# The turned v of a fused attention and feed-forward kernel: from TensorE to transposing DMAs, and the pace of the second half's units

## Chip, cores and metric

The kernel runs on one core of one Trainium2 chip. The metric is the device time of one execution in microseconds (us), lower being better. The kernel before was timed five times; its median is 241.97 us, and the five times lie between 241.94 and 242.24 us.

## What is computed

The reference first turns `sort_net` into one 8x8 block-mixing matrix P for each of the 32 heads (4 batches of 8 heads). It then mixes the eight 96-row blocks of k and v with P, runs softmax attention block by block, and feeds the result to a bilinear feed-forward layer:

```
P: five times exp, then rows and columns divided by their sums
k_sorted = einsum('bhij,bhjcd->bhicd', P, k_blocks)     # 8 blocks of 96 rows, 64 wide
v_sorted = einsum('bhij,bhjcd->bhicd', P, v_blocks)
attn     = softmax(scale * q_block @ k_sorted_block.T)  # 96 x 96 for each block
o        = attn @ v_sorted_block
x        = o with heads side by side                    # 3072 tokens x 512
out      = ((x @ w_a) * (x @ w_b)) @ w_out              # 512 -> 1536 -> 512
```

## The kernel before

**Tiling.** Heads are worked on in pairs: a pair's two 64-wide heads fill 128 partitions. There are 16 pairs, numbered g = 0 to 15, four to a batch. A pair passes through stage c (mix k and v), stage s (scores and exp) and stage o (attention times v, division by the row sums). Four finished pairs make up xT, the transposed input of one batch's feed-forward layer. A step `ffn_ab` of that layer is eight 384-column matmuls on TensorE (four with w_a, four with w_b), a copy of the first product by ScalarE and a multiply by VectorE; `ffn_out` multiplies with w_out and stores.

**What v needs.** The mix gives v with the head dimension on the partitions (vT). The o matmul wants the 96 tokens of a block on the partitions (vs), so every block of vT is transposed. The kernel before does it in two ways. For batch 0 and for pair 4, the first pair of batch 1, TensorE does it: `half_v` (line 205) transposes four blocks of a pair into PSUM and VectorE copies them to vs (line 211); `turn_v` (line 269) does the same for all eight blocks of pair 4. For pairs 5 to 15 `return_v` (line 316) issues one transposing DMA, SBUF to SBUF, on the queue of SyncE (SP).

**Order of work.** The order on TensorE, GpSimd (POOL) and SP is the order in which the program is written. Batch 0 is treated in two halves of its blocks, h = 0 and h = 1, so that the feed-forward layer can begin early. Half 0 is written out by hand (lines 499 to 529). The twelve units of half 1 come from `units_half` (line 547) and are laid between the twelve `ffn_ab` steps of half 0 by `interleave` (line 628). For each pair hp they are: `half_scores` with `half_v` right behind it, in one unit; `half_o`; and `half_x`, which transposes the result on TensorE and copies it into xT. `half_x` of a pair is placed behind a later step than its `half_o`. With one step kept free at the end and two at the beginning, `interleave` has placed ceil((s-1) x 12 / 9) units once the step of index s is done. After that come steps that share TensorE with the pairs of batch 1 (`paced`, line 637, in the order of line 604: c4, s4, c5, s5, c6, o4, s6 ...). The last two unit kinds wait for other engines: `half_o` for ScalarE's exp (line 202), `half_x` for VectorE's reciprocal and multiply (lines 237 and 239).

**Buffers.** There are four vT tiles, one for each pair of a batch, and three vs tiles used in turn (g modulo 3). In the PSUM pool psF, four banks serve the feed-forward products, the transposes of v and x, and the first mixes.

**DMA.** POOL issues all loads with a cast to bf16 (`load_ab` line 105: w_a and w_b in six column chunks of 256, two steps of the layer each; `load_pair` line 88; `load_out` line 111: w_out in three parts). SP issues the stores and the transposing DMAs: `stage_q` (line 252) for the q of later pairs, `return_v`, and `to_xT` (line 341). SP takes them strictly in turn, and each waits there for its inputs.

Of the kernel before, what the change touches and what calls it, by code (L numbers as in the profile page):

```python
# [10 lines left out]
BF16 = mybir.dt.bfloat16  # L11
# [11 lines left out]
def kernel(  # L23
# [11 lines left out]
    nc = tc.nc  # L35
    P = 128
    B, H, S, D = q.shape
    NB = sort_net.shape[-1]
    BLK = S // NB
# [7 lines left out]
    HP = H // 2  # L47
    KA = DMODEL // P
    KO = DFF // P
    NBH = NB // 2  # L50
# [4 lines left out]
    V0 = 16  # L55
# [12 lines left out]
    psF = ctx.enter_context(tc.tile_pool(name="psF", bufs=4, space=PSUM))  # L68
# [5 lines left out]
    ident = const.tile([P, P], BF16, name="ident")  # L74
# [50 lines left out]
    NBUF = 3  # L125
    kTs = [const.tile([P, S + PAD], BF16, name=f"kT{n}") for n in range(HP)]
    vTs = [const.tile([P, NB, P], BF16, name=f"vT{n}") for n in range(HP)]
    eTs = [const.tile([BLK, 2, 2, HB + PAD], BF16, name=f"eT{n}") for n in range(NBUF)]
    vss = [const.tile([P, NB, VW], BF16, name=f"vs{n}") for n in range(NBUF)]
# [29 lines left out]
    def copy(eng, out, in_):  # L159
        if eng == "act":  # L160
            nc.scalar.copy(out=out, in_=in_)  # L161
        else:
            nc.vector.tensor_copy(out=out, in_=in_)  # L163

    def keep_busy(ps, n, cols=512):
        for _ in range(n):
            nc.tensor.matmul(ps[:, 0:cols], lhsT=warm[:, 0:P], rhs=warm[:, 0:cols],  # L167
                             start=True, stop=True)


    def mix_mms(g, what, where):
        src2 = loaded[g][0 if what == "k" else 1]
        for c in range(NCH):
            for e in range(2):
                nc.tensor.matmul(where(c)[e * D:(e + 1) * D], lhsT=src2[:, e, c * D:(c + 1) * D],  # L175
                                 rhs=s_all[:, 2 * g + e], start=True, stop=True)

    def mix_first(g, what, engines, fill=0, cols=512):
        mix = [psF.tile([P, 512], FP32, tag="F", name="mixf") for _ in range(2)]
        keep_busy(mix[0], fill, cols)  # L180
        mix_mms(g, what, lambda c: mix[c // 3][:, c % 3 * P:(c % 3 + 1) * P])
        for u, eng in enumerate(engines):
            copy(eng, turned(g, what, u),
                 _ap(mix[u], 0, [[512, P], [P, 3], [CG, NB], [1, CG]]))

    def turned(g, what, u):
        if what == "k":
            return _ap(kTs[g % HP], u * 3 * CG, [[S + PAD, P], [CG, 3], [BLK, NB], [1, CG]])
        return _ap(vTs[g % HP], u * 3 * CG, [[NB * P, P], [CG, 3], [P, NB], [1, CG]])

    def half_scores(h, hp):
        g = h * HP + hp
        kT, qT, eT = kTs[hp], st[hp, "qT"], eTs[g % NBUF]
        sc = psA.tile([P, 2, 512], FP32, tag="A", name="sc")
        for i in range(NBH):
            for e in range(2):
                nc.tensor.matmul(  # L197
                    sc[:, e, i * BLK:(i + 1) * BLK],
                    lhsT=kT[e * D:(e + 1) * D, (h * NBH + i) * BLK:(h * NBH + i) * BLK + P],
                    rhs=qT[e * D:(e + 1) * D, :, (h * NBH + i) * CG:(h * NBH + i + 1) * CG],  # L200
                    start=True, stop=True)
        nc.scalar.activation(out=eT[:, 0, :, 0:HB], in_=sc[0:BLK, :, 0:HB],  # L202
                             func=AF.Exp, scale=float(scale))

    def half_v(h, hp):
        g = h * HP + hp
        vT, vs = vTs[hp], vss[g % NBUF]
        vs_ps = psF.tile([P, NBH, 2, D], BF16, tag="F", name="vs_ps")
        for i in range(NBH):
            nc.tensor.matmul(vs_ps[:, i], lhsT=vT[:, h * NBH + i], rhs=ident, is_transpose=True)  # L210
        nc.vector.tensor_copy(out=vs[0:BLK, 0:NBH, V0:V0 + P],
                              in_=vs_ps[0:BLK].rearrange("p i e d -> p i (e d)"))

    def half_o(h, hp):
        g = h * HP + hp
        xp = att.tile([BLK, NBH, 2, D], BF16, tag="xph", name="xph")
        one_o(eTs[g % NBUF], 0, vss[g % NBUF], 0, xp, NBH)
        st["x", h, hp] = xp

    def half_x(h, hp, eng):  # L220
        xT, xp = xT_of(0), st["x", h, hp]
        xt_ps = psF.tile([P, NBH, BLK], BF16, tag="F", name="xt_ps")
        for i in range(NBH):
            nc.tensor.matmul(xt_ps[:, i, :], lhsT=xp[:, i],  # L224
                             rhs=ident[0:BLK, 0:BLK], is_transpose=True)
        copy(eng, xT[:, hp, h * HW:(h + 1) * HW].rearrange("p (i t) -> p i t", i=NBH), xt_ps)
# [30 lines left out]
    def turn_q(g, eng="dve"):  # L257
# [7 lines left out]
        qT = qtp.tile([P, NCH, P], BF16, tag="qT", name="qT")  # L265
        copy(eng, qT, q_ps)
        st[g, "qT"] = qT

    def turn_v(g):
        vT, vs = vTs[g % HP], vss[g % NBUF]  # L270
        vs_ps = psF.tile([P, NB, P], BF16, tag="F", name="vs_ps")
        for i in range(NB):
            nc.tensor.matmul(vs_ps[:, i], lhsT=vT[:, i], rhs=ident, is_transpose=True)
        nc.vector.tensor_copy(out=vs[0:BLK, :, V0:V0 + P], in_=vs_ps[0:BLK])

    def stage_k(g):
        mix = psA.tile([P, 2, 512], FP32, tag="A", name="mix")
# [13 lines left out]
    def plain(g):  # L291
        return g >= 2 * HP + 2
# [23 lines left out]
    def return_v(g):  # L316
        nc.sync.dma_start_transpose(out=vss[g % NBUF][:, :, V0:V0 + P],
                                    in_=vTs[g % HP].rearrange("p i t -> p (i t)"))
# [105 lines left out]
    with tc.manual_schedule(engines={ET.PE, ET.Pool, ET.SP}):  # L424
        with tc.manual_schedule(engines={ET.Activation, ET.DVE}):
# [7 lines left out]
            for it in range(5):  # L433
# [8 lines left out]
                if it == 2:  # L442
                    with nc.allow_low_precision("sum of one one and zeros"):
                        nc.vector.reduce_sum(
                            out=mask, in_=_ap(ident, 0, [[P, P], [1, CG], [CG, NB]]),
# [14 lines left out]
                else:  # L460
                    nc.vector.tensor_mul(
                        out=p_fin.bitcast(BF16).rearrange("h (i j u) -> h i j u", i=NB, j=NB),
# [30 lines left out]
            def partial(n, *kcs):  # L493
                if n not in begun:
                    begun[n] = (psF.tile([P, 512], FP32, tag="F", name="pf") if n < 3 else
                                psA.tile([P, 2, 512], FP32, tag="A", name="two")[:, 0])
                ab_mms(begun[n], (w_a_sb, w_b_sb)[n % 2], 0, n // 2, 0, kcs)
# [3 lines left out]
            mix_first(1, "v", ("act", "dve"), 1)  # L501
            mix_first(1, "k", ("act", "dve"))
            half_scores(0, 0)
            half_v(0, 0)
            mix_first(2, "v", ("act", "dve"))
            mix_first(2, "k", ("act", "act"))
            half_o(0, 0)
            half_scores(0, 1)
            half_v(0, 1)
            half_v(0, 2)  # L510
            mix_first(3, "k", ("dve", "act"))
            half_scores(0, 2)
            half_o(0, 1)
            mix_first(3, "v", ("act", "act"))
            half_x(0, 0, "dve")
            half_o(0, 2)
            half_x(0, 1, "act")
            half_scores(0, 3)
            partial(0, 0)
            half_v(0, 3)  # L520
            partial(0, 1)
            half_x(0, 2, "dve")
            half_o(0, 3)
            partial(4, 0, 1, 2)
            partial(2, 0, 1, 2)
            partial(0, 2)
# [18 lines left out]


        def units_half():
            def R(hp):
                half_scores(1, hp)
                half_v(1, hp)  # L550

            us = []
            for hp in range(HP):
                us.append(lambda hp=hp: R(hp))
                if hp > 0:
                    us.append(lambda hp=hp: half_x(1, hp - 1, "dve"))
                us.append(lambda hp=hp: half_o(1, hp))
            us.append(lambda: half_x(1, HP - 1, "dve"))
            return us

        def c_(g):
            if g < 2 * HP - 2:
                turn_q(g)
            if plain(g):
                stage_plain(g, "k", ("act",))
                stage_plain(g, "v", ("dve", "act"))
            else:
                stage_k(g)
                stage_v(g)
            if plain(g):  # L570
                pair_q(g)
                stage_q(g)
            else:
                if g > HP:
                    return_v(g)
                if g >= 2 * HP - 2:
                    nc.gpsimd.tensor_copy(out=gate, in_=kTs[g % HP][0:1, 0:1])  # L577
                    load_later(g)

        def s_(g):  # L580
            stage_scores(g)
            if g == HP:
                turn_v(g)
            if g in (HP, HP + 1):
                stage_q(g + 2)
            if 2 * HP <= g + 1 < B * HP and not plain(g + 1):
                pair_q(g + 1)
                stage_q(g + 1)
# [20 lines left out]
        for n, (b, u, g) in enumerate(seq):  # L609
            if u is c_ and plain(g):  # L610
                late = 3 if g % HP == 0 else 2
                after[n + 1] += [lambda g=g, what=what: in_order(g, what) for what in "kv"]
                if late == 3:
                    after[n + 3].append(lambda g=g: nc.gpsimd.tensor_copy(
                        out=gate, in_=xT_of(g // HP - 1)[0:1, HP - 1, 0:1]))
# [8 lines left out]
        units = [[] for _ in range(B)]  # L624
# [3 lines left out]
        def interleave(steps, units, spare, first):  # L628
            n, done = len(steps) - spare - first, 0
            for s, step in enumerate(steps):  # L630
                step()
                want = -(-(s + 1 - first) * len(units) // n)
                while done < min(want, len(units)):
                    units[done]()
                    done += 1
# [53 lines left out]
```

The softmax here doesn't subtract the row's maximum and nothing guards it: scores larger than these inputs give would overflow.

## Time and profile before

| | |
|---|---|
| median of five runs | 241.97 us |
| the profiled execution's own time | 242.03 us |
| its span, first to last instruction | 240.2 us |
| TensorE (PE) busy | 233.7 us, 97% of the span |
| VectorE (DVE), ScalarE (ACT) busy | 111.2 us and 101.3 us |
| transposing DMAs on SP's queue | 45: 11 vs, 10 q, 12 k and v of later pairs, 12 xT |
| `half_v`: PE transposes, DVE copies | 32 of 219 ns each, 8 of 416 ns each |
| `turn_v`: PE transposes, DVE copy | 8 of 220 ns each, 1 of 687 ns |

About 1.8 us of the execution lie outside the span. PE is matmul, PEld the loading of weights into TensorE ahead of a matmul. Matmuls overlap in TensorE, so 219 ns is how long one took from start to end; how long it holds up the next is read from the distance of starts. "Waits" tell which engine or DMA ended an engine's idle time, and "issue" is time for which the profile shows no cause. "To landing" is the time from a DMA's issue to its completion. All times are counted from the start of the span.

### The profile page before, as it was taken

To read this page: it belongs to the slowest core of one execution; us is meant where nothing else is said; L and a number is where in the kernel's file an instruction comes from. 1 tells how busy PE (TensorE), PEld (TensorE's weight loads), DVE (VectorE), ACT (ScalarE), POOL (GpSimd) and SP (SyncE) were. 2 spreads that over 40 slices of the span, in tenths; PEclk is the share of its full clock that TensorE was granted. 3 is DMA by queue.
4 is the path that set the end of the run, shared out by engine and by line. 5 is a ranking of instruction groups with operands and counts; after the bars stand their busy time and mean duration, and the time that the engine had idled before them with its cause. 6 is when DMAs were issued, how large, how long until landed. Compare 5 with 4: busy or idle time off the path is not lost.

```text
span 240.2 us, 5193 instructions
## 1 busy us (share of the span) xinstructions
PE 233.7 (97%) x2091; PEld 138.8 (58%) x2091; DVE 111.2 (46%) x262; ACT 101.3 (42%) x187; POOL 70.4 (29%) x97
## 2 busy tenths in 40 slices
PE   7899899999999999999999999999999999999994
PEld 7776566666554466666645455666544466665443
DVE  6797667546345144365406244644544134444110
ACT  3774634664630165743640356455500133333001
POOL 8776569623320055071620515411000000000000
PEclk9999999999999999999999999999999999999999
DMA  5999999995998589769995899975325200000132
GB/s 77 202 199 196 196 200 201 202 166 98 151 151 205 125 120 160 120 104 197 155 202 109 160 252 100 151 142 35 76 61 140 101 30 3 0 0 3 44 130 88
DMA packets 63527, 30.35 MB, mean 126 GB/s; under 512 B 40336, under 2 KB 60560, under 8 KB 63504
## 3 DMA queue, kind: packets, MB, share of 16 engines
q0 software_dynamic: 20944, 14.16, 42.2%
q1 hardware_dynamic: 42416, 15.81, 34.2%
q8 instruction: 16, 0.26, 0.4%
q10 hardware_dynamic: 144, 0.07, 0.1%
q14 instruction: 7, 0.06, 0.1%
HBM read 28.32 MB, written 6.29 MB: 144 GB/s over the span
## 4 chain that ended last, share of the span: by engine, by line
PE 92%; DVE 4%; ACT 1%; DMA 1%; issue 1%; DVEq 0%; ACTq 0%
PE pf L357 52%; PE po L402 24%; PE o_ps L233 3%; PE sc L327 2%; PE mix L175 2%; PE mix L298 2%; PE mixf L175 1%; PE po L387 1%; PE sc L197 1%; PE vs_ps L210 1%; DMA p_nat<-in_sort_net_dram 1%; PE xt_ps L224 1%; DVE csum L455 1%; PE two L357 1%; DVE xp L239 1%
## 5 line engine op out<-in xcount | busy, mean ns | idle before, releaser
L378 DVE TENSOR_TENSOR hT<-a_sb,pf 128x384 bf16<-128x384 bf16 x95 | 52.6, 553 | 71.6 <-PE pf L357 45.2
L357 PE MATMUL pf<-xT,w_a_sb 128*128 128x384 bf16 x380 | 78.0, 326 | 0.0
L357 PE MATMUL pf<-xT,w_b_sb 128*128 128x384 bf16 x380 | 77.4, 326 | 0.0
L377 ACT CAST a_sb<-pf 128x384 bf16<-128x384 f32 x95 | 45.4, 479 | 63.2 <-PE pf L357 39.9
L402 PE MATMUL po<-w_out_sb,hT 128*128 128x512 bf16 x276 | 61.9, 379 | 0.0
L357 PEld LDWEIGHTS <-w_b_sb 128*128 128x128 bf16 x384 | 37.5, 98 | 24.7
L357 PEld LDWEIGHTS <-w_a_sb 128*128 128x128 bf16 x384 | 35.3, 98 | 22.4
L402 PEld LDWEIGHTS <-hT 128*128 128x128 bf16 x276 | 26.2, 97 | 30.2
L161 ACT COPY o_sb<-po 128x512 f32<-128x512 f32 (+1 forms) x13 | 7.5, 578 | 48.9 <-PE po L402 47.5
L163 DVE COPY o_sb<-po 128x512 f32<-128x512 f32 (+1 forms) x12 | 7.9, 658 | 38.7 <-PE po L402 34.1
L332 ACT ACTIVATE eT<-sc 96x768 bf16<-96x768 f32 x24 | 18.1, 802 | 5.2 <-PE sc L327 5.2
L239 DVE TENSOR_TENSOR xp<-o_ps,rec 96x512 bf16<-96x512 f32 x24 | 15.9, 684 | 0.3
L314 POOL COPY kT<-turned 128x768 bf16<-128x768 bf16 x6 | 5.0, 827 | 33.5 <-DMA turned<-nat 28.0
L233 PEld LDWEIGHTS <-eT 96*128 96x128 bf16 x256 | 10.2, 97 | 4.4 <-ACT eT L202 1.1
L96 POOL DMA_DIRECT2D k<-in_k_dram x16 | 11.6, 724 | 3.5 <-PE pf L357 1.3
L96 POOL DMA_DIRECT2D v<-in_v_dram x16 | 11.6, 722 | 2.8 <-DMA w_b_sb<-in_moe_w_b_dram 1.3
L233 PE MATMUL o_ps<-vs,eT 96*128 96x65 bf16 x256 | 11.4, 193 | 1.0 <-ACT eT L202 0.6
L577 POOL COPY gate<-kT 1x1 bf16<-1x1 bf16 x4 | 0.7, 178 | 32.2 <-ACT kT L280 27.7
L161 ACT CAST nat<-mix 128x768 bf16<-128x768 f32 (+1 forms) x12 | 7.7, 639 | 4.2 <-PE mix L298 2.5
L248 POOL COPY qc<-q 128x768 bf16<-128x768 bf16 x10 | 8.5, 846 | 2.6 <-DMA q<-in_q_dram 2.6
L96 POOL DMA_DIRECT2D q<-in_q_dram x12 | 8.7, 724 | 1.5 <-DMA w_a_sb<-in_moe_w_a_dram 0.6
L167 PE MATMUL heat<-warm 128*128 128x128 bf16 x84 | 7.4, 259 | 1.3 <-DVE warm L77 1.3
(86 smaller groups left out, 163.8 us busy)
## 6 DMA issues: line engine op xcount, KB each, us to landing
out_dram<-o_sb SPq DMA_DIRECT2D x17, 256.0 KB, 2.0
k<-in_k_dram POOLq DMA_DIRECT2D x16, 192.0 KB, 5.5
v<-in_v_dram POOLq DMA_DIRECT2D x16, 192.0 KB, 6.1
q<-in_q_dram POOLq DMA_DIRECT2D x12, 192.0 KB, 6.5
w_a_sb<-in_moe_w_a_dram POOLq DMA_DIRECT2D x6, 256.0 KB, 9.0
w_b_sb<-in_moe_w_b_dram POOLq DMA_DIRECT2D x6, 256.0 KB, 9.5
w_out_sb<-in_moe_w_out_dram POOLq DMA_DIRECT2D x3, 512.0 KB, 12.1
out_dram<-o_sb SPq DMA_DIRECT2D x12, 128.0 KB, 2.4
```

The lines of the kernel that those rows point to most:

```text
L96: nc.gpsimd.dma_start(out=to, in_=_ap(t, base, [[W, P], [S * D, 2], [1, W]]))
L161: nc.scalar.copy(out=out, in_=in_)
L163: nc.vector.tensor_copy(out=out, in_=in_)
L167: nc.tensor.matmul(ps[:, 0:cols], lhsT=warm[:, 0:P], rhs=warm[:, 0:cols], start=True, stop=True)
L233: nc.tensor.matmul(o_ps[:, e, i * (D + 1):(i + 1) * (D + 1)], lhsT=eT[:, hf, e, i * BLK:i * BLK + P], rhs=vs[0:BLK, i0 + i, V0 - 1 + e * ( ...
L239: nc.vector.tensor_tensor(out=_ap(xp, i0 * 2 * D, [[nxp * 2 * D, BLK], [D, 2], [2 * D, NBH], [1, D]]), in0=_ap(o_ps, 1, [[1024, BLK], [511 ...
L248: nc.gpsimd.tensor_copy(out=qc.rearrange("p c e d -> p e c d"), in_=loaded[g][2].rearrange("p e (c d) -> p e c d", c=NCH))
L332: nc.scalar.activation(out=eT[:, hf, :, 0:HB], in_=sc[0:BLK, :, 0:HB], func=AF.Exp, scale=float(scale))
L357: nc.tensor.matmul(pf[:, 0:HW], lhsT=w_sb[:, kc, m * P:(m + 1) * P], rhs=x_cols(b, kc, t), start=(kc == 0), stop=(kc == KA - 1))
L377: nc.scalar.copy(out=a_sb, in_=pf[:, 0:HW])
L378: nc.vector.tensor_mul(out=hT[:, m, t * HW:(t + 1) * HW], in0=a_sb, in1=ab[1][:, 0:HW])
L402: nc.tensor.matmul(held["po"], lhsT=hTs[b][:, m, c * P:(c + 1) * P], rhs=w_out_sb[:, m, :], start=(m == 0), stop=(m == KO - 1))
```

## The change

Half 1 of batch 0: the new `second_v(hp)` issues one transposing DMA on SP's queue, which turns blocks 4 to 7 of the pair's vT into the vs tile that half 1 of the pair will read. It is issued as soon as the previous reader of that vs tile has been written down: `second_v(0)`, `(1)` and `(2)` behind `half_o(0, 1)`, `(0, 2)` and `(0, 3)` in the hand-written part, `second_v(3)` behind `half_o(1, 0)`. The four `half_v(1, hp)` are gone. Pair 4: `turn_v` is gone, and `return_v(4)` is issued in stage c like those of the later pairs. The units of half 1 are in a new order, in which scores run one pair ahead, and `interleave` rounds the number of units down where it rounded up.

```diff
+    def second_v(hp):
+        nc.sync.dma_start_transpose(out=vss[(HP + hp) % NBUF][:, 0:NBH, V0:V0 + P],
+                                    in_=vTs[hp][:, NBH:].rearrange("p i t -> p (i t)"))
+
-    def half_v(h, hp):
-        g = h * HP + hp
-        vT, vs = vTs[hp], vss[g % NBUF]
+    def half_v(hp):
+        vT, vs = vTs[hp], vss[hp % NBUF]
...
-            nc.tensor.matmul(vs_ps[:, i], lhsT=vT[:, h * NBH + i], rhs=ident, is_transpose=True)
+            nc.tensor.matmul(vs_ps[:, i], lhsT=vT[:, i], rhs=ident, is_transpose=True)
...
-    def turn_v(g):
...
             half_o(0, 1)
+            second_v(0)
             mix_first(3, "v", ("act", "act"))
             half_x(0, 0, "dve")
             half_o(0, 2)
+            second_v(1)
             half_x(0, 1, "act")
             half_scores(0, 3)
             partial(0, 0)
-            half_v(0, 3)
+            half_v(3)
             partial(0, 1)
             half_x(0, 2, "dve")
             half_o(0, 3)
+            second_v(2)
             partial(4, 0, 1, 2)
...
         def units_half():
-            def R(hp):
-                half_scores(1, hp)
-                half_v(1, hp)
-
-            us = []
+            def O(hp):
+                half_o(1, hp)
+                if hp == 0:
+                    second_v(HP - 1)
+
+            us = [lambda: half_scores(1, 0)]
             for hp in range(HP):
-                us.append(lambda hp=hp: R(hp))
+                if hp + 1 < HP:
+                    us.append(lambda hp=hp: half_scores(1, hp + 1))
                 if hp > 0:
                     us.append(lambda hp=hp: half_x(1, hp - 1, "dve"))
-                us.append(lambda hp=hp: half_o(1, hp))
+                us.append(lambda hp=hp: O(hp))
             us.append(lambda: half_x(1, HP - 1, "dve"))
             return us
...
-                if g > HP:
-                    return_v(g)
+                return_v(g)
...
             stage_scores(g)
-            if g == HP:
-                turn_v(g)
...
-                want = -(-(s + 1 - first) * len(units) // n)
+                want = (s + 1 - first) * len(units) // n
```

The units of half 1 behind each `ffn_ab` step, with S for `half_scores`, V for `half_v`, O for `half_o` and X for `half_x` (steps 0, 1 and 11 have none in either kernel):

| step | 2 | 3 | 4 | 5 | 6 | 7 | 8 | 9 | 10 |
|---|---|---|---|---|---|---|---|---|---|
| before | S0 V0 O0 | S1 V1 | X0 | O1 S2 V2 | X1 | O2 | S3 V3 X2 | O3 | X3 |
| after | S0 | S1 | O0 S2 | X0 | O1 | S3 X1 | O2 | X2 | O3 X3 |

More of the change, by code (lines that the diff above doesn't have):

```diff
@@ L267, in turn_q @@
         st[g, "qT"] = qT
-    def turn_v(g):
[L270 to L274, printed above, removed]
     def stage_k(g):
@@ L503 @@
             half_scores(0, 0)
-            half_v(0, 0)
+            half_v(0)
             mix_first(2, "v", ("act", "dve"))
@@ L508 @@
             half_scores(0, 1)
-            half_v(0, 1)
-            half_v(0, 2)
+            half_v(1)
+            half_v(2)
             mix_first(3, "k", ("dve", "act"))
```

## Prediction

> **What bounds the kernel now.** I read the page first, then the chain of waits, the timeline where the change sits, and last the DMA's landings.
>
> The page says TensorE:
>
> ```profile
> PE 233.7 (97%) x2091; PEld 138.8 (58%) x2091; DVE 111.2 (46%) x262; ACT 101.3 (42%) x187; POOL 70.4 (29%) x97
> DMA  5999999995998589769995899975325200000132
> ```
>
> PE has work in 97% of the span. The second line is the DMA's share in slices of 6 us: it is full from 6 us to about 54 us, and that is where the change puts five more transfers. So I need both: what TensorE saves, and whether the new transfers come in time on a full DMA.
>
> The chain around the first unit of half 1 (start, length, what):
>
> ```profile
> 25.36 0.36 PE sc L197 x8
> ...
> 25.80 0.81 ACT eT L202
> 26.62 0.05 issue
> 26.66 0.42 PE o_ps L233 x8
> ```
>
> S0, V0 and O0 come in one go, and O0 waits for the exp. V0 starts at 25.64 in the timeline and takes 0.23, so O0 could start at 25.87 and starts at 26.66: PE stands still for 0.79 us.
>
> The timeline of O3 and X3, with one step between them:
>
> ```profile
> 38.86 0.41 PE L233 MATMUL o_ps<-vs,eT 96*128 96x65 bf16 x8
> ...
> 39.83 0.69 DVE L239 TENSOR_TENSOR xph<-o_ps,rec 96x512 bf16<-96x512 f32 x1
> ...
> 40.57 0.20 PEld L224 LDWEIGHTS <-xph 96*128 96x128 bf16 x4 [0.39 <-DVE xph L239]
> 40.58 0.34 PE L224 MATMUL xt_ps<-ident,xph 96*128 96x96 bf16 x4
> ```
>
> From O3's start to X3's is 1.72 us: VectorE finishes a product, then the reciprocal and the multiply. O3 takes 0.25 (the step starts at 39.11) and the step 1.30, so X3 waits 0.17.
>
> The third view is the tile qTf, whose first transposing DMA met the full DMA:
>
> ```profile
> L254 SPq DMA_TRANSPOSE qTf<-qc x10: 1212/1306/2238, 42.8 to 161.1; - x10
> DMA to landing us min/median/max: 2.6/4.2/10.5
> ```
>
> The reader is to see the longest: 10.5 us from issue to landing, against a median of 4.2. It is the first of the ten, issued at 42.78 on the full DMA and landed at 53.30.
>
> [...]with nothing else under way (54.5 to 55.0 us) I count 545 packets of 256 bytes in the trace's packet records, 279 GB/s; beside the loads of w_out, 155 packets in a us, 40 GB/s. [...]from 47 to 50 us 463 of POOL's and 468 of SP's, one for one.
>
> **The change part by part.**
>
> TensorE transposes. V1 runs from 28.59 to the next step at 28.83, V2 from 32.22 to 32.45, V3 from 37.15 to 37.38, V0 took 0.23: 0.92 us of PE for four. turn_v: 46.43 to 46.89, 0.46 us. All of it is on PE, which is the bound: -1.38. The five VectorE copies that go (4 x 0.42 and 0.69 us) count 0: VectorE is busy 46% of the span and its copies lie beside PE's matmuls. If VectorE were the limit there, they would bring up to 2.4 us more.
>
> The new order. S0 and O0 are two steps apart: -0.79. S1 to S3 keep their places behind a step or an O. O0 to X0 has S2 and a step between, O1 to X1 a step and S3, 1.9 us each against the 1.4 (O0 before, VectorE free) to 1.72 that VectorE takes: 0; without S2 or S3 each would cost 0.17. O2 to X2 is now a pair like O3 and X3 before, one step apart: +0.17; the old X3 wait goes: -0.17. O3 and X3 now follow each other behind step 10, with nothing between: 1.72 less O3's own 0.25, +1.47. What is late next behind X3 is its copy into xT, which the next batch of steps reads; step 11 (1.30 us) covers it, as now.
>
> Sum for TensorE: -1.38 - 0.79 - 0.17 + 0.17 + 1.47 = -0.70. At c4 the shift is -0.24, from o4 on -0.70.
>
> SP's queue. It now holds second_v(0) to (3), then return_v(4), then stage_q(6), which stood first and went out at 42.78. An issue takes about 1.25 us of SP (the vs rows). second_v(3) waits at the head for O0; behind it there is only return_v(4), over 15 us later: 0. stage_q(6) goes behind return_v(4), at about 47.
>
> second_v in time? (0) can go when half_o(0,1) is done, 18.45; (1) 19.7; (2) 21.55; (3) about 29.2. 512 packets each. Under load the first packets came 3.4 to 3.9 us after the issue (qTf 42.78, 46.7; xT 59.67, 63.1). A transposing packet beside POOL's costs these about 1.5 ns: w_out alone goes at 200 packets a us, paired at 155 (1/155 - 1/200). The chunks of w_a and w_b go alone at 390 a us, so paired at about 243, an estimate. Then (0) lands by 25.5 and is read at O0 near 28.6; (1), (2) and (3) have 3 us and more. The change makes each O's weight load wait for these landings, and all of TensorE's later work is queued behind it, so if the slack is gone, each us late is a us lost; I take 0, with a pause of 0.85 (below) too. The copies of vT at c4 on VectorE and ScalarE now wait for the landings as well, as they overwrite what is being turned: 44 us against 25 to 35, 0.
>
> What they do to the loads. 1536 packets x 1.6 ns (1/243 - 1/390) put POOL's loads back by 2.4 us, with second_v(3) and slower pairs 3.2. The first that matters is chunk 1 of w_a: landed at 21.21, read at 21.34. A first transposing packet at 20.8 instead of 22 would cost up to 0.4; none, 0. I take 0.15. The other chunks have over 2 us, but for chunk 2 of w_b (landed 25.02, now 27.4, read about 28.1): 0, up to 0.9 with a pause. Pair 4 (36.0, read at 43.5), pair 5 and w_out have 4 us or more.
>
> return_v(4). The copies of vT (ScalarE's 45.28 + 0.48) end at 45.76, with c4's shift and w_a's wait (-0.24 + 0.15) at 45.67. Its data is read by o4, whose weights are loaded from
>
> ```profile
> 57.21 0.36 PEld L233 LDWEIGHTS <-eT 96*128 96x128 bf16 x5
> ```
>
> now at 57.21 - 0.70 + 0.15 = 56.66. Its first packets go out about 3.6 us after the issue, 49.2, when w_out is being loaded (put back by 3.2 us, to 48.0 and later). 1024 packets at 155 a us are 6.6 us, and a landing came 0.8 after the last packet: 56.6. That is just in time. But the DMA stopped in that very stretch before, and the table of stretches of 2 us shows it in its last column:
>
> ```profile
> 48.00:50.00 2.00, 2.00 (x26) 1.20 (x25) 0.79 (x2) 0.96 (x2) 1.61 (x1) 1.00 1.24 204
> 50.00:52.00 2.00, 2.00 (x36) 1.31 (x31) 1.34 (x3) 1.39 (x3) 0.00 (x0) 1.00 1.37 119
> ```
>
> 204 GB/s fall to 119: from 50.7 to 51.6 hardly a packet starts. Up to 46 us, loads alone, there was no such pause after the first 5 us; with both queues busy (46 to 54 us) there were two. I take one of 0.85 for return_v(4): +0.85, with ends 0 and 1.7.
>
> stage_q(6) follows on the same ring with 768 packets. Two us of them share with w_out's rest, the others run alone or beside pair 8's loads: it lands between 59.5 and 61.8. s6 reads it at 60.56 - 0.70 + 0.15 + 0.85 = 60.86. Cost 0 to 0.9; I take 0.40. return_v(5) and stage_q(7) then have 2 us or more.
>
> Sum: -0.70 + 0.15 + 0.85 + 0.40 = +0.70. Against the profiled execution 242.03 + 0.70 = 242.73; it lies 0.06 above the median of the runs, 241.97, so 242.67, say 242.7.
>
> **The rivals.**
>
> The crossbar keeps up. For it: 56.6 against 56.66 without a pause, and slack everywhere else. Against it: the pauses. Time: 241.97 - 0.70, with 0 to 0.15 for w_a: 241.3 to 241.4, faster. This is the one on the other side; it decides at a pause of about 0.1 us before return_v(4)'s last packet.
>
> A wait at o4 alone, part of a pause or a whole one, after which stage_q(6) is in time: for it speaks that s6 comes later by o4's wait, against it that 768 packets still stand behind return_v(4). -0.70 + 0.15 + 0.5 to 0.85, 241.9 to 242.3, no change.
>
> Late weights. Pauses come in the first stretch already, where 1536 new packets share with w_a and w_b, and chunk 2 of w_b holds up step 4: +0.9, with 0.85 at o4: 243.1 to 243.5. Against it: the small chunks have shown no pause so far, though alone.
>
> The unit order does not do what it says: "evenly" puts O3 and X3 together. That is in the sum; without it all cases were 1.47 lower.
>
> **How the numbers follow.** Forecast 0.37 (242.5 to 243.1), late weights 0.09, a wait at o4 alone 0.29, the crossbar in time 0.25. A measurement of this kernel can tell about 0.2%, 0.48 us, from no change, so the bounds are 241.49 and 242.45. Faster 0.25, same 0.29, slower 0.46. The range reaches from the fast rival's 241.3 to 243.4 and leaves out the end of the late weights and what I haven't seen. The forecast's own range is 242.45 to 243.1.
>
> **What would show it.** Right: no wait of O0 for eT; PE idle about 1.5 us before X3, released by VectorE's xph; PE waiting for the DMA vs<-vT before o4 near 57, with return_v(4) landing 11 us or more after its issue; a smaller wait before s6 for qTf<-qc. Wrong: return_v(4) landing under 10 us, or no PE wait for a DMA at all: then it is near 241.3. Also wrong if second_v's packets go out of turn with the loads, so that O0 waits for its vs, or if X3's wait is under 1 us.

## The result and the profile after

The kernel after takes 245.03 us, the median of 27 runs (242.58 to 248.88), against 242.12 for 48 runs of the kernel before (241.83 to 243.22). The ratio of the comparison is 1.0061, with a 95% interval of 1.0046 to 1.0076: slower, by more than the 0.2% that can be told from no change. That ratio leaves out the eleven runs over 246.2 us, all of them at a TensorE clock of 0.986 to 0.993 (the profile below, one of them, shows the low clock right behind the kernel's own wait); with every run the ratio of the two medians is 1.012. The forecast, 242.7 us with 241.3 to 243.4, has the right sign, and the median lies outside it.

The profiled execution took 248.75 us with a span of 246.7. It is a bad one of the 27, but the two other profiles of the same kernel (`after_again`, 245.37 us, and `after_third`, 242.65 us) show the same wait, of other lengths.

First the page of the kernel after. The last two lines are groups: busy time and mean ns, then idle time and what ended most of it.

```profile
PE 234.2 (95%) x2067; PEld 137.9 (56%) x2067; DVE 109.2 (44%) x257; ACT 100.9 (41%) x187; POOL 70.4 (29%) x97
...
PEclk9999999999799999999999999999999999999999
DMA  5999999999999949958998798953227310000132
...
L236 PE MATMUL o_ps<-vs,eT 96*128 96x65 bf16 x256 | 11.4, 193 | 4.1 <-DMA vs<-vT 3.8
...
L236 PEld LDWEIGHTS <-eT 96*128 96x128 bf16 x256 | 10.2, 97 | 7.8 <-DMA vs<-vT 4.2
```

PE falls from 97 to 95% of a longer span. The DMA is now full to about 86 us (14 slices of 6.17 us), where it was full to 54, and the o matmul waits for a DMA into vs. One slice of the clock, the 11th (62 to 68 us), isn't full.

The chain at half 1's first units, in the kernel after:

```profile
26.61 0.35 PE sc L197 x8
26.96 1.41 PE pf L353 x8
28.36 0.28 PE sc L197 x8
28.64 1.41 PE pf L353 x8
30.05 0.25 PE o_ps L236 x8
```

Where S0 was followed by 0.81 us of exp, the chain runs through TensorE alone, and O0 takes 0.25 us in place of 0.42. O0 waits neither for eT nor for the turned v.

The timeline of O3 and X3 in the kernel after:

```profile
39.89 0.41 PE L236 MATMUL o_ps<-vs,eT 96*128 96x65 bf16 x8
...
41.60 0.20 PEld L227 LDWEIGHTS <-xph 96*128 96x128 bf16 x4 [1.43 <-DVE xph L242]
41.61 0.34 PE L227 MATMUL xt_ps<-ident,xph 96*128 96x96 bf16 x4 [1.31 <-DVE xph L242]
```

From O3's start to X3's it is 1.72 us, as before, with no step between: PE is idle for 1.3 us. Of the rest of the new order only X2 holds PE up, by 0.17 us, as forecast: it starts at 38.41, 1.72 after O2.

The chain that ends at o4, in the three profiles of this kernel, first the one of the page, then `after_again`, then `after_third`:

```profile
46.82 15.03 DMA vs<-vT
61.84 0.05 issue
61.89 0.67 PE o_ps L236 x16
```

```profile
46.13 14.02 DMA vs<-vT
60.15 0.05 issue
60.19 0.67 PE o_ps L236 x16
```

```profile
45.49 11.92 DMA vs<-vT
57.41 0.05 issue
57.46 0.67 PE o_ps L236 x16
```

The middle column is return_v(4) from its issue to its landing: 15.0, 14.0 and 11.9 us. The forecast had 10.9 without a stop of the DMA and 11.8 with the one that it took, so the third profile meets it. c4 to o4 takes 13.47 us where nothing waits (44.00 to 57.47 in `rv4_only`, below). Here it takes 17.41, 16.40 and 14.30, so o4's wait costs 3.94, 2.93 and 0.83 us.

The stretches around o4 in the kernel after (busy time of PE, PEld, DVE, ACT and POOL, then the granted clock, DMA share, GB/s):

```profile
58.00:60.00 2.00, 0.12 (x1) 0.00 (x0) 0.55 (x1) 0.21 (x1) 1.97 (x3) 1.00 1.29 171
60.00:62.00 2.00, 0.11 (x4) 0.11 (x5) 0.00 (x0) 0.00 (x0) 0.00 (x0) 1.00 1.40 80
62.00:64.00 2.00, 2.00 (x22) 1.26 (x21) 1.56 (x4) 0.17 (x1) 0.00 (x0) 0.64 1.72 140
64.00:66.00 2.00, 2.00 (x8) 0.91 (x6) 0.56 (x1) 0.30 (x1) 0.00 (x0) 0.51 1.55 105
66.00:68.00 2.00, 2.00 (x26) 1.17 (x25) 0.55 (x1) 1.32 (x3) 0.00 (x0) 1.00 1.33 196
```

PE stands still for 3.8 us; then the clock is 0.50 for 3.4 us (62.5 to 66.0, in whole stretches 0.64 and 0.51), and o4 to s6 takes 4.88 us in place of 3.19. In `after_again`, where PE waits 2.8 us, the clock stays full:

```profile
58.00:60.00 2.00, 0.00 (x0) 0.00 (x0) 0.10 (x1) 0.00 (x0) 1.28 (x2) 1.00 1.43 125
60.00:62.00 2.00, 1.81 (x25) 1.29 (x25) 1.31 (x4) 0.40 (x1) 0.00 (x0) 1.00 1.33 190
```

There o4 to s6 takes 3.21 us, and 3.20 in `after_third`. So the half clock is a cost of its own, 1.69 us, which of the three profiles only the one with the longest wait shows.

The account of the page's profile against the one of before, 248.75 - 242.03 = 6.72 us: a later S0, 26.61 against 25.36, +1.25; S0 to c4 -0.22; turn_v -0.45; o4's wait +3.94; the half clock +1.69; the time from the last matmul's start to the span's end +0.2; outside the span +0.3. The sum is 6.71. The later S0 comes from the first loads: the first mixes wait for a v that lands at 16.50, before the first new transfer is even issued (19.76). In `after_third` S0 is at 25.29, and the sum there is -0.07 - 0.22 - 0.45 + 0.83 + 0.22 + 0.31 = +0.62, measured 242.65 - 242.03.

### The profile page after: what moved, and what is told of

The parts are those of the page before. It is cut to its first block, busy times and chain, and to the rows that moved or that the text cites. A ratio compares the mean times of both kernels' runs of the same rounds, so it can differ in the third digit from the quotient of the medians.

```text
span 246.7 us, 5165 instructions
## 1 busy us (share of the span) xinstructions
PE 234.2 (95%) x2067; PEld 137.9 (56%) x2067; DVE 109.2 (44%) x257; ACT 100.9 (41%) x187; POOL 70.4 (29%) x97
## 4 chain that ended last, share of the span: by engine, by line
PE 84%; DMA 10%; POOL 2%; DVE 2%; issue 0%; POOLq 0%; DVEq 0%
PE pf L353 48%; PE po L398 24%; DMA vs<-vT 6%; DMA v<-in_v_dram 4%; PE o_ps L236 3%; PE sc L323 2%; PE mix L294 2%; PE mix L175 1%; PE po L383 1%; POOL k L96 1%; PE sc L197 1%; PE xt_ps L227 1%; PE mixf L175 1%; POOL q_first L83 1%; POOL v L96 1%; PE two L353 1%
## 5 line engine op out<-in xcount | busy, mean ns | idle before, releaser
L353 PE MATMUL pf<-xT,w_a_sb 128*128 128x384 bf16 x380 | 79.1, 330 | 0.0
L240 DVE RECIPROCAL rec<-o_ps 96x8 f32<-96x8 f32 x32 | 5.6, 189 | 8.9 <-PE o_ps L236 8.7
```

What stands on the lines that cost most here:

```text
L240: nc.vector.reciprocal(out=rec, in_=_ap(o_ps, 0, [[1024, BLK], [512 + D, 2], [D + 1, NBH]]))
L353: nc.tensor.matmul(pf[:, 0:HW], lhsT=w_sb[:, kc, m * P:(m + 1) * P], rhs=x_cols(b, kc, t), start=(kc == 0), stop=(kc == KA - 1))
```

## Experiments

Three theories stood at the start. A: return_v(4) meets the load of w_out (POOL's last before the later pairs) whatever second_v does, and its landing decides o4. B: it is second_v, whose 2048 packets put the loads back, and return_v(4) comes in time without it. C: the new order of the units holds the time. After the first four runs came A2: only both together are late, since second_v puts w_out back to where it covers the whole of return_v(4)'s transfer. The runs called `..._apart` also put O3 and X3 apart.

### The kernel after once more: `after_again`, `after_third`

> The changed kernel once more, with a profile of its own. Theory A (the loss is made at o4, where TensorE waits for the late return_v(4) on a full DMA, and grows by TensorE's halved clock once that wait is long): the time scatters again between 242.6 and 249 us, and in the profile the wait of o4 for vs<-vT explains it: time = 241.4 us + wait, plus up to 1.7 us of slow clock[...]. Theory B (second_v's four transfers put all loads back, and TensorE waits for weights and pairs in several places): several waits for loads of w_a, w_b, k or v of over 0.3 us between 20 and 60 us. Theory C (the loss is in the order of the units): PE's waits before X2 and X3 together make over 2 us.

> The changed kernel a third time, one look, for the spread of o4's wait. Theory A2: the profile's time is 242.0 us plus o4's wait (TensorE's -0.67, and +0.57 that runs with second_v showed outside TensorE's work), plus 1.7 us if the wait is so long that the clock halves; a time of 242.7 us goes with a wait of 0.7 us, one of 245 with 3. If the wait doesn't follow the time, something else spreads it.

`after_again`: 244.98 us, median of four (244.35 to 247.49), ratio 1.0130 (1.0087 to 1.0173). `after_third`: one run, 242.65. Their chains stand above. The wait is there each time, 0.8 to 3.9 us. The runs of this kernel differ by 6.3 us, those of before by 1.4; of the 6.1 us between the longest and the shortest profile 3.1 are the wait, 1.7 the half clock behind it and 1.3 the later S0.

### Pair 4 back on TensorE: `pair4_te`

```diff
-                return_v(g)
+                if g > HP:
+                    return_v(g)
...
             stage_scores(g)
+            if g == HP:
+                turn_v(g)
```

> The changed kernel, but pair 4's v turned by TensorE as before; half 1 still on the crossbar and in the new unit order. Theory A: no wait for a transposing DMA at o4, TensorE sum -0.24 us against before, with w_a's chunk up to +0.4: 241.8 to 242.4 us, scatter as small as before's. Theory B: second_v's transfers are still there, so most of the loss stays: over 243 us. Theory C: the order is still there, so the loss stays too: over 243 us.

Measured 242.42 us (14 runs), ratio 1.0010 (0.9999 to 1.0020). PE doesn't wait for a DMA at o4. So neither second_v alone nor the new order alone makes the loss: without return_v(4) it is gone. The loads are late here too: pair 7's q lands at 48.78 against 44.81 before, w_out's last part at 58.37 against 54.45.

### return_v(4) alone: `rv4_only`

The kernel before, with the opposite of that edit and nothing else.

> The kernel before, but pair 4's v turned by return_v(4) on the crossbar instead of TensorE; half 1 untouched. Theory A: TensorE sum -0.46 us, and o4 waits for return_v(4), which meets w_out's load as in the changed kernel: 242.5 to 247 us, with scatter. Theory B: without second_v the loads come 3 us earlier, return_v(4) lands in time (by 56.7 us in the trace): 241.4 to 241.7 us. Theory C: nothing of the order is in it: 241.4 to 241.7 us.

Measured 241.75 us (14 runs), ratio 0.9984 (0.9971 to 0.9997). A falls: return_v(4) meets w_out and still comes in time. The tile vs in this profile, the transposing DMAs from SP and their landings:

```profile
L317 SPq DMA_TRANSPOSE vs<-vT x4: 1235/1284/2163, 46.3 to 64.5; - x4
...
DMA to landing us min/median/max: 4.4/5.6/8.6
```

Issued at 46.33, landed at 54.94, 8.6 us, with o4 at 57.47. The packet records say why. w_out's packets fall from 158 a us at 50 to 58 at 51, for that load is nearly through, and the transposes then go at 300 to 700 a us. In `after_third` w_out keeps to 150 or 160 a us up to 57, but for a stop at 51, and so do the transposes, one for one. The tile w_out_sb gives the same in one line each, first before, then `after_third`:

```profile
L112 POOL DMA_DIRECT2D w_out_sb<-in_moe_w_out_dram x3: 777/785/787, 39.2 to 40.6; - x3
...
DMA to landing us min/median/max: 8.3/12.1/13.8
```

```profile
L112 POOL DMA_DIRECT2D w_out_sb<-in_moe_w_out_dram x3: 777/785/787, 43.1 to 44.6; - x3
...
DMA to landing us min/median/max: 9.6/12.3/14.9
```

The last part is issued at 40.6 and lands at 54.4 before; in `after_third` at 44.6 and 59.5. return_v(4) runs beside a load that ends five us later.

### w_out loaded later: `wout_late`

```diff
-        for c in range(3):
-            load_out(c)
...
         pair_q(2 * HP - 2)
         pair_q(2 * HP - 1)
+        for c in range(3):
+            load_out(c)
```

> The changed kernel, but GpSimd issues the three loads of w_out behind its two copies of q for pairs 6 and 7 instead of ahead of them, so that return_v(4) goes out when the DMA has little else to do. Theory A: return_v(4) lands within 8 us of its issue, o4 doesn't wait, and TensorE's sum of -0.70 us (+0.15 for w_a's chunk) is left: 241.3 to 241.6 us with small scatter. Theory B: the loads before w_out are as late as in the changed kernel: over 242.5 us. Theory C: over 242.5 us.

Measured 246.94 us (six runs), ratio 1.0186 (1.0157 to 1.0215): a miss. return_v(4) does land in 5.9 us (45.53 to 51.39), and o4 doesn't wait. But the waits of this profile between 66 and 80 us show where the loss went:

```profile
PE o_ps L236 <- DMA vs<-vT: 2.4, 1, 2.4
...
PE sc L323 <- DMA qTf<-qc: 1.2, 1, 1.2
```

The next two transposing DMAs met w_out instead: return_v(5) took from 51.22 to 64.35, the q of pair 7 from 52.92 to 68.17. SP's own issues for vs took up to 5.4 us each, so return_v(7) went out at 67.52 (64.42 before) and landed at 75.61. The waits are at s7, for that q, and at o7. The bytes are the same, and delaying this load passed the wait on. The expectation had looked at o4 alone. The profile, 245.19 us, is the fastest of the six; the other five are at a clock of 0.992 or 0.993.

### Half 1's v on TensorE, the rest as after: `v2_te`

```diff
-            second_v(0)
...
-                if hp == 0:
-                    second_v(HP - 1)
...
+            def R(hp):
+                half_scores(1, hp)
+                half_v(1, hp)
...
-            us = [lambda: half_scores(1, 0)]
+            us = [lambda: R(0)]
```

> The changed kernel, but half 1's v turned by TensorE (no second_v); pair 4's return_v(4) and the new unit order stay. Theory A2 (second_v's packets put the loads back by 4 us or more, and only that makes return_v(4) share with w_out for its whole length and come late): return_v(4) lands by 56 us in the trace, o4 doesn't wait; TensorE sum -0.46 - 0.79 + 1.47 = +0.22 us: 242.2 to 242.5 us with small scatter. Rival C2 (the new order, with its dense end, makes return_v(4) late or costs elsewhere): o4 still waits by over 1 us, over 243.5 us.

Measured 242.18 us (13 runs), ratio 1.0005 (0.9996 to 1.0013). return_v(4) lands 8.6 us after its issue, as in `rv4_only`. S0 to c4 takes 18.77 us against 18.09 before, +0.68; the prediction's terms without the four transposes are -0.79 - 0.17 + 0.17 + 1.47 = +0.68. That is what is to be said of C: the order costs what X2 and X3 wait, less what O0 and the old X3 waited, and nothing more.

### One second_v only: `one_v2`

```diff
+            def R(hp):
+                half_scores(1, hp)
+                if hp < HP - 1:
+                    half_v(1, hp)
```

`v2_te` with this, and second_v(3) kept.

> The changed kernel, but of half 1 only the last pair's v (second_v(3)) is on the crossbar, the other three are on TensorE; return_v(4) and the new order stay. Theory A2, in which the amount put ahead of the loads decides: 512 packets put them back by about 1 us, return_v(4) lands by 56.5 us in the trace, o4 doesn't wait: 242.0 to 242.6 us. If any crossbar transfer among the loads is enough (a pause of the DMA that one transfer brings as well as four): o4 waits over 1 us, over 243.2 us.

Measured 242.05 us (14 runs), ratio 0.9999 (0.9986 to 1.0012). Pair 7's q lands at 46.56 and w_out at 55.77, return_v(4) at 56.35 (9.75 us after its issue), and o4, at 57.74, doesn't wait. So it isn't that a transfer stands ahead of return_v(4), but how far all of them put the loads back: w_out lands at 53.48 with none, 55.77 with one, 58.37 to 62.00 with four.

### O3 and X3 apart: `order_only`, `pair4_xbar_apart`, `v2_xbar_apart`

The call of `interleave` becomes a call of `placed`, which writes the listed units behind the step named, with a step between every O and its X, and S0 and O0 two steps apart. `unit_s` is `half_scores` (with `half_v` where v is turned on TensorE), `unit_o` and `unit_x` are `half_o` and `half_x`.

```diff
+placed(steps, {2: [(unit_s, 0)], 3: [(unit_s, 1)],
+               4: [(unit_o, 0), (unit_s, 2)],
+               5: [(unit_x, 0), (unit_o, 1)],
+               6: [(unit_s, 3), (unit_x, 1)], 7: [(unit_o, 2)],
+               8: [(unit_o, 3)], 9: [(unit_x, 2)], 10: [(unit_x, 3)]})
```

`order_only` is the kernel before with that list; `pair4_xbar_apart` is that with return_v(4); `v2_xbar_apart` is the kernel after with the list (O3 behind step 9) and turn_v. "On the crossbar" means by transposing DMA.

> The kernel before, with nothing on the crossbar but what was there, and half 1's units placed by hand (scores with v two steps ahead of O, no O directly ahead of its X). Theory A2: the two waits of TensorE go, -0.79 - 0.17 = -0.96: 241.0 to 241.3 us, and the difference to the run that has pair 4 on the crossbar too (240.6 us) is turn_v's 0.46. If the crossbar's part in that run were more than turn_v's time: over 241.4 us.

> Pair 4's v on the crossbar, half 1's v on TensorE as in the kernel before, and half 1's units placed by hand: scores with their v two or more steps ahead of their O, no O directly ahead of its X. TensorE sum against before: -0.46 for turn_v, -0.79 for O0's wait, -0.17 for X3's wait = -1.42. Theory A2: return_v(4) in time, so 240.5 to 240.9 us, under both kernels. Rival C2: running scores ahead makes return_v(4) late, over 242 us.

> Half 1's v on the crossbar as in the changed kernel, pair 4's v on TensorE, and half 1's units placed by hand so that O3 and X3 have a step between them (O3 and X2 behind step 9, X3 behind step 10). Against the run with pair 4 on TensorE and the changed order (242.4 us): theory A2 has X3's wait as plain TensorE time, so 1.3 us less: 241.0 to 241.3 us. If that wait is covered by something later, as rival C2 would need, the time stays at 242.2 to 242.5 us.

| kernel | us, median (runs) | ratio, 95% interval | S0 to c4, us | c4 to o4, us |
|---|---|---|---|---|
| `order_only` | 241.16 (14) | 0.9961 (0.9949 to 0.9973) | 17.12 | 13.92 |
| `pair4_xbar_apart` | 240.59 (5) | 0.9937 (0.9925 to 0.9949) | 17.11 | 13.47 |
| `v2_xbar_apart` | 241.30 (22) | 0.9975 (0.9962 to 0.9988) | 16.48 | 13.92 |

S0 to c4 takes 18.09 us before, so the order alone brings 0.97, which is O0's 0.79 and X3's 0.17; return_v(4) brings its 0.45 on top; and the four transposes by DMA bring 0.64 more than on TensorE up to c4, with a short new wait of X3 inside (38.92, 1.82 us after O3). But `v2_xbar_apart` is slower than its gain of 1.61 says: its tail, from the start of the last matmul to the end of the span, is 0.25 longer, and 2.10 us lie outside the span in place of 1.8. And six of its 22 runs take 242.27 to 245.63 us, the last at a clock of 0.993. So with four second_v something is late in some executions even where pair 4 is on TensorE; the one profile, 240.93 us, doesn't show what. `pair4_xbar_apart` is faster than both kernels. Its chain at the end of the layer and at o4:

```profile
38.32 0.17 PE xt_ps L224 x4
38.49 1.30 PE pf L357 x8
39.80 0.17 PE xt_ps L224 x4
...
56.14 0.49 PE o_ps L233 x16
```

X2 and X3 take 0.17 us each, and no DMA stands ahead of o4.

### PE kept busy through the wait: `kept_busy`

```diff
+            if g == HP:
+                keep_busy(psF.tile([P, 512], FP32, tag="F", name="idle"), 18)
```

The kernel after, with 18 matmuls ahead of o4 that nobody reads.

> The changed kernel with 18 matmuls of 512 columns on a tile of zeros (3.9 us) ahead of o4, so that TensorE works while it would wait for return_v(4). If the slow clock behind o4 comes of TensorE's idle time: no stretch of halved clock any more, granted clock 1.00 in all runs, the time between 244.5 and 246 us with a scatter under 1.5 us. If the slow clock has another cause: runs with a clock of 0.99 and times of 247 to 249 us are still among them.

Measured 245.83 us (four runs, 245.57 to 246.38), ratio 1.0153 (1.0139 to 1.0168), every run at a clock of 0.999 or more. The stretches after the wait in this profile:

```profile
60.00:62.00 2.00, 2.00 (x26) 1.32 (x25) 0.89 (x3) 0.00 (x0) 0.00 (x0) 1.00 1.57 153
62.00:64.00 2.00, 2.00 (x20) 1.10 (x20) 1.27 (x5) 0.96 (x2) 0.00 (x0) 1.00 1.49 145
```

The clock stays at 1.00, and o4 to s6 takes 3.19 us. In this execution return_v(4) was early (57.62), so the idle matmuls themselves, which end at 60.6, held o4 up: as a remedy it is worth nothing. It also means that this profile is no direct counterpart to the one with 0.64 and 0.51: with its landings at 57.41 (`after_third`) and 60.15 (`after_again`) the kernel after kept its clock at 1.00 too. What speaks for PE's idle time as the cause is that none of four executions falls under 0.999, where eleven of 27 of the kernel after do, and that 246.38 us with a full clock is among them, where every run of the kernel after from 246.33 us up has a lower one. Four runs agree with it; they don't prove it.

### Four transposes more, where nobody waits: `four_more`

```diff
+            if g == B * HP - 1:
+                for n in range(HP):
+                    nc.sync.dma_start_transpose(
+                        out=vss[n % NBUF][:, 0:NBH, V0:V0 + P],
+                        in_=vTs[n][:, NBH:].rearrange("p i t -> p (i t)"))
```

The kernel before with these, behind the last xT.

> The kernel before, with four transposing DMAs of half 1's size added on SP behind the last one that turns x (about 183 us), where the DMA is nearly idle; nobody reads what they write. It tests the 0.57 us that the runs with second_v showed outside TensorE's work (0.27 between the last matmul and the end of the span, 0.3 outside the span). If it belongs to the number of transposing DMAs: +0.3 to +0.6 us, 242.4 to 242.7 us. If it belongs to where second_v stands: 242.0 to 242.2 us.

Measured 242.26 us (22 runs), ratio 1.0012 (1.0004 to 1.0020). From the start of the last matmul to the end of the span it takes 3.57 us, against 3.32 before and 3.52 to 3.59 in the kernels with four second_v. So that part of the tail, 0.25 us, comes with four transposing DMAs more, behind the last xT here and among the first loads with second_v; one or two more (`rv4_only`, `v2_te`, `one_v2`) don't bring it, 3.22 to 3.28. The time outside the span stays at 1.77 us and isn't explained by it.

## Why the prediction was wrong, step by step

**TensorE's sum, -0.70: right.** S0 to c4 was to change by -0.24 and changed by -0.22 (18.09 to 17.87 in `after_again`); turn_v was to bring 0.46 and brings 0.45. O0's wait is gone, X3 starts 1.72 us after O3, and `v2_te` and `order_only` give the terms +0.68 and -0.97 by themselves.

**second_v in time, 0: right.** In `after_third` the four land at 25.25, 28.48, 30.64 and 35.76 us, each 2.8 us or more ahead of its O (O0 starts at 28.6), and no o_ps of half 1 waits for vs in any profile.

**w_a's first chunk, +0.15, and chunk 2 of w_b: not seen.** From the first mix to the first product with w_a nothing changes in the profiles that start like before. Chunk 2 of w_b lands at 27.41 in `after_third`, where 27.4 was forecast, and PE waits for no load there, though a stop of the DMA falls into that stretch, as the rival of the late weights had it. `after` and `after_again` start half 1 late by 1.25 and 0.56 us, but by a v awaited before any new transfer is issued; `rv4_only` does so by 0.55 us without second_v. Whether the change has any part in that was not tried.

**What second_v does to the loads, 3.2 us: mis-sized.** Pair 7's q lands at 48.99 in `after_third` against 44.81 before, 4.2 us later, and at 48.78 in `pair4_te`. Of that some 0.8 us is one stop of the DMA between 26 and 29 us, seen in each profile with four second_v. The rest is 3.4 us or 1.6 to 1.7 ns for each of 2048 packets: the price was right, the stop was missing.

**return_v(4), +0.85 with ends 0 and 1.7: this is the step that failed.** Its last term, 0.8 us from the last packet to the landing, was mis-sized. The transfer's three parts, by the packet records (its 1024 packets counted in the order in which SP's queue starts them):

| us | forecast | `after_third` | `after_again` | `after` |
|---|---|---|---|---|
| issue to first packet | 3.6 | 3.87 | 3.86 | 4.15 |
| first to 1024th packet | 6.6 + 0.85 | 7.40 | 7.82 | 7.98 |
| 1024th packet to landing | 0.8 | 0.65 | 2.34 | 2.89 |
| together | 11.8 | 11.92 | 14.02 | 15.02 |

The first two parts are as forecast or each up to 0.6 us longer: the queues share at 150 to 160 packets a us, and there is one stop. (The prediction's 463 and 468 packets from 47 to 50 us come out as 468 and 469 here, which changes nothing.) The third part was taken as fixed, from the kernel before, so the range allowed for stops and for nothing else. Two of the three profiles have 2.3 and 2.9 us in its place.

stage_q(6) follows on the same queue, so in `after` the 1024th packet need not be the last of return_v(4). In `after_again` that hardly matters. In the records each transposing DMA ends with 32 packets of 4 bytes; the 32nd starts at 58.08, and by then only 86 packets of stage_q(6) have started, so nearly all of return_v(4) is out. It lands 2.1 us later. In `after_third` it lands 0.35 us after the 32nd.

What these 2 us wait for is not shown. In `after_third` return_v(4) lands two us ahead of the last of w_out (57.41 against 59.47), and its 16 completion signals come within 0.3 us. In the other two it lands only with w_out, 60.15 against 60.62 and 61.84 against 62.01, and its signals are spread over 1.8 and 2.1 us. In that time w_out's last packets trickle out, at 68 a us and fewer. I take it that some of the 16 DMA engines finish return_v(4) only when they are nearly through with w_out; the records don't name the engine, so this is argued. In the kernel before, the transfer that met w_out landed over a us ahead of it (53.30 against 54.45), so its profile showed no such case.

With the landing 0 to 1.7 late, the range ended at 243.4; o4's wait was up to 3.94.

**Where the forecast fits, part of it is chance.** Eight of the 27 runs lie between 242.58 and 242.92, and `after_third` took 242.65. Its wait at o4, 0.83, is the forecast's 0.85. But the 0.15 of w_a and the 0.40 of stage_q(6) aren't in it; 0.53 us behind the last matmul and outside the span, which were not counted, stand in their place.

**The cause is an interaction.** return_v(4) alone brings 0.16% (0.9984), the kernel with second_v and the new order but not return_v(4) is at most 0.2% slower than before (`pair4_te`), half 1's v on TensorE takes the loss away too (`v2_te`), and only both together lose 0.6 to 1.3%. One reservation is the six long runs of `v2_xbar_apart`, which has second_v without return_v(4). The prediction had both on its list and added them. Its "crossbar in time" is what `rv4_only` and `pair4_xbar_apart` show, in kernels where w_out isn't put back.

**What was not counted.** A half clock behind the longest wait, 1.69 us. The profiles give two points: after 2.8 us of waiting PE in `after_again` the clock stayed at 1.00, after 3.8 us in `after` it was 0.50 for 3.4 us. What lies between them was not shown, and that PE's idle time is the cause rests on the four runs of `kept_busy`. The forecast's longest wait, 1.7 us, lies below both points, so this follows from the failed step. Then the tail's 0.2 to 0.27 us and 0.3 us outside the span (about 2.10 us in `after`, `kept_busy`, `wout_late` and `v2_xbar_apart`, 1.91 in `pair4_te`, about 1.8 in the kernels with one second_v or none): small, but as large as the margins between the forecast's cases.

**stage_q(6), +0.40: not seen.** o4 to s6 takes 3.20 and 3.21 us at full clock, the same as without the change. Its q lands 0.7 us ahead of s6 in `after_third` (59.98 against 60.66) and 2.3 and 4.3 us ahead in the other two, where o4's wait has moved s6 back. The prediction named this against it, as one of its rivals: the wait at o4 alone.

**Left open:** why return_v(4) lands 2 us after its last packet in some executions and not in others, and so why o4's wait is 0.8 us in one and 3.9 in another; what makes six runs of `v2_xbar_apart` long; and the 0.3 us outside the span. The kernel after with O3 and X3 apart and return_v(4) kept was not run.

## What to carry to other kernels

A transfer that is moved onto a full DMA is to be costed with the other moved transfers in place, not beside the kernel as it was: here the four early ones put the end of w_out's load from 54.4 us to between 58.4 and 62.0, and return_v(4), which in `rv4_only` met that load when it was nearly through, shared with it over nearly its whole length. Where a landing has no slack left, the number to look for is how long the two queues will run side by side, since sharing held this transposing DMA to 155 packets a us, where with w_out nearly through (`rv4_only`) it had 300 to 700, and whether its end falls together with the load's. And a gain of the order of units was had without any transfer: a step between O3 and X3 and two between S0 and O0 brought 0.4%, and with one of the five transfers 0.6%.

## What was not expected of the hardware

The two DMA queues went packet for packet at two pairs of packet sizes. In `after` from 56 to 57 us 155 packets of w_out's queue (nearly all of 1024 bytes) and 155 of return_v(4) (256 bytes) start; from 30 to 31 us 249 of the loads' queue (nearly all of 512 bytes) and 250 of second_v (256 bytes). So return_v(4) moves 40 GB/s beside w_out, and in `rv4_only` 300 to 700 packets a us (77 to 179 GB/s) as soon as that load is nearly through.

Delaying w_out shortened return_v(4) from 11.9 us (`after_third`) to 5.9 (`wout_late`). Of the two transposing DMAs behind it return_v(5) took 13.1 us in place of 9.1, and the q of pair 7 took 15.

In two of the three profiles of the kernel after, return_v(4) ended together with w_out, and late. In `after_again` it landed 2.1 us after nearly all of its packets had started, next to the last of w_out; in `after_third`, where it was through two us ahead of w_out, it took 0.35 us.

Four transposing DMAs that no engine waits for made the time after the last matmul 0.25 us longer (3.57 us in `four_more`, 3.32 before). It is 3.52 to 3.59 with the four second_v too, which are issued at 18 to 30 us, over 200 us before the end.
